# Zeros on TensorE before the first tokens, and a paced preparation, in an attention and mixture kernel

## The chip, the cores and the metric

The kernel runs on one core of one Trainium2 chip, in one launch. The metric is device time in microseconds (us), the median of several runs.

## What is computed

Two blocks follow each other. The first is a causal attention with decay in 8 heads; it has no softmax, so it is computed with a running state per head:

```python
for b in range(nb):                       # blocks of 64 positions of q, k, v [4, 8, 768, 64]
    intra = einsum('bhic,bhjc->bhij', qb, kb) * Dmask     # powers of lam below the diagonal
    intra = einsum('bhij,bhjd->bhid', intra, vb)
    inter = einsum('bhid,bhde->bhie', qb * lam_pow, kv_state)
    out[:, :, sl] = intra + inter
    kv_state = lam_block * kv_state + einsum('bhsd,bhse->bhde', kb * rev_pow, vb)
```

Its output, laid out as x [3072, 512], goes through four experts, whose results are weighted by normalised probabilities:

```python
p = domain_probs / (domain_probs.sum(-1, keepdims=True) + 1e-09)
for e in range(4):                        # w1 [4, 512, 1024], w2 [4, 1024, 512], float32
    h = np.maximum(x @ w1[e], 0.0)
    out += p[:, e:e + 1] * (h @ w2[e])
```

## The kernel before

The tokens are cut into chunks of 128 and three groups of eight chunks (group 0, 1, 2). A unit is one group with one expert: twelve units. The products of a unit are made by Strassen's scheme, seven products M1 to M7 of half-size blocks in place of eight, and each of the seven is again split so. What enters them are the blocks A11 to A22 of a weight, B11 to B22 of the tokens, and sums of those (S1 to S4, T1 to T4). The sums of weights and tokens are made on GpSimd and VectorE ahead of time, written to DRAM (`w1_ops`, `x_ops`, `w2_sums`, `w2_ops`) and fetched when their product comes.

The program writes out every engine's order itself. It starts with the loads, all issued by SyncE (SP) in this order:

```python
for n, names in ((0, "qk"), (1, "qk"), (0, "v"), (2, "qk"), (1, "v")):
    load(n, names)
raw_w1(0, "A11")
load(3, "qk")
load(2, "v")
raw_w1(0, "A12")
load(3, "v")
raw_w1(0, "A21")
raw_w1(0, "A22")
```

A chunk passes through three functions. `turn` transposes q and k on TensorE (`qp`, `kp`), ScalarE copies the results out, and GpSimd decays k. `scores` multiplies them (`sp`), VectorE masks. `values` makes the output (`op`) and the new state, which VectorE writes to `kv`; ScalarE copies the output to `xT`, the tokens of the group. For group 0 the chunks run through a loop, and quarters of the first two products of unit 0 (M1 and M2, from raw weights) stand between:

```python
between = {
    4: (m1[0], m1[2]), 5: (m2[0], m2[2]), 6: (m1[1],), 7: (m1[3],), 8: (m2[1],),
    9: (lambda: None, lambda: None, m2[3]),
}
for i in range(CPG + 2):                   # CPG = 8
    if i > 5:
        pump()
    more = list(between.get(i, ()))
    for f, lag in ((scores, 1), (turn, 0), (values, 2)):
        n = i - lag
        if 0 <= n < CPG:
            f(n, pairs[n % 3])
        if i == 9 and lag == 2:
            x_sums()                       # T1 to T4 of the tokens, VectorE
        if more:
            more.pop(0)()
    if i + 4 < CPG:
        load(i + 4)
```

Then come the other five products of unit 0, in quarters (`direct_product`, tile `pM`; M5 is the third). Preparation is a list of small jobs, `chores`. Each call of `pump` does one of them, and issues the stores of the one before the last:

```python
def pump():
    for f in older:
        f()
    older[:] = stores
    stores.clear()
    if chores:
        chores.pop(0)()
```

The rest is the loop over units. In each of its seven steps one product of the next unit's first layer (`a`, tile `pg`, operands `xs_in` and `ws_in`) and one of this unit's second layer (`b`, tile `q` with weights `w2t`; in the last group, nested once more, tile `pq`) are interleaved in parts. VectorE adds each part to its sum when TensorE has ended it, and so frees the PSUM bank. For unit 1 the preparation `own(m)` makes the sums of tokens on VectorE and those of weights on GpSimd just before use:

```python
for at, (g, e) in enumerate(units):
    ...
    for i in range(7):
        for _ in range(2 if at + i == 0 else 1):
            if fill2:
                feed2(*fill2.pop(0))       # loads w2t of this or the next product
        ...
        if nested:
            order = [a[0:2], b[0:2], a[2:4], b[2:4], a[4:6], b[4:6], a[6:8], b[6:8]]
        else:
            order = [a[0:2], b[0:1], a[2:4], b[1:2], a[4:6], b[2:3], a[6:8], b[3:5]]
        for x, part in enumerate(order):
            for f in part:
                f()
            ...
            if x == 0 and at * 7 + i >= 6 and fill:
                feed(*fill.pop(0))         # loads xs_in, ws_in of the next product
            if steps and (at > 0 or i > 1) and (x == 5 or (x == 2 and i in (1, 3, 5) and at > 0)):
                steps.pop(0)()             # attention of the next group
            if x % (2 if g == 0 else 3) == 0:
                pump()
```

Of the kernel before, what the change touches and what calls it, by code (L numbers as in the profile page):

```python
# [21 lines left out]
def kernel(  # L22
# [30 lines left out]
    nc = tc.nc  # L53
# [39 lines left out]
    def tt(eng, o, a, b, op):  # L93
        eng.tensor_tensor(out=o, in0=a, in1=b, op=op)  # L94

# [35 lines left out]


    chores, stores, older, made = [], [], [], set()

    def pump():
        for f in older:
            f()
        older[:] = stores
        stores.clear()
        if chores:  # L140
            chores.pop(0)()

    def nothing():
        pass

    def until(what):
        while what not in made:
            pump()

    def inner(eng, what, to, blk, ops, at):  # L150
# [6 lines left out]
        stores.append(lambda: (  # L157
# [24 lines left out]
    def weight_steps(block, total, ready):  # L182
        return [
            lambda: (block("A11", 0, 0), block("A21", 1, 0), block("A22", 1, 1)), nothing, nothing,
# [32 lines left out]
    def prepare_w2(e):  # L217
# [8 lines left out]
        def total(name, n, a, b, op):  # L226
# [3 lines left out]
            stores.append(lambda: (  # L230
# [6 lines left out]
            lambda: (block("B12", 0, 1), block("B22", 1, 1)), nothing,  # L237
# [11 lines left out]
    def inner_w2(e, m, blk):  # L249
# [6 lines left out]
        stores.append(lambda: (  # L256
# [80 lines left out]
    for n, names in ((0, "qk"), (1, "qk"), (0, "v"), (2, "qk"), (1, "v")):  # L337
        load(n, names)
    raw_w1(0, "A11")
    load(3, "qk")  # L340
# [3 lines left out]
    raw_w1(0, "A21")  # L344
    raw_w1(0, "A22")
# [61 lines left out]
    now = [0]  # L407
# [107 lines left out]
    def attention(g):  # L515
# [3 lines left out]
        for n in range(g * CPG, (g + 1) * CPG):  # L519
# [3 lines left out]
            def end(n=n):  # L523
                values(n, ("s0", "s1"))
# [161 lines left out]
    def first_product(g, e, m, blocks, tags):  # L686

        while (g, e, m) not in fed:
            pump()
# [55 lines left out]
    def second_product(g, e, m, banks):  # L745

        def part(sj, s):
# [29 lines left out]
            if e == E - 1 and m in ("M2", "M4", "M5", "M3"):  # L777
                stores.append(lambda: nc.sync.dma_start(out=out[n * P:(n + 1) * P, j * DH:(j + 1) * DH], in_=o))
# [218 lines left out]
    def keep_own(what, to, pieces):  # L997
        def store():
            for (x, y), of in pieces:
                nc.sync.dma_start(out=to[:, x:y], in_=of)  # L1000
            made.add(what)

        stores.append(store)
# [35 lines left out]
    def x_sums():  # L1039
        for name, a, b in (("T1", "B12", "B11"), ("T2", "B22", "T1"), ("T3", "B22", "B12"), ("T4", "B21", "T2")):  # L1040
            t = stream.tile([P, 7, 256], FP32, name="xt", tag="xw"[len(x_now) % 2])
            x_tile[name] = t
            x_now[name] = t[:, 0:4].rearrange("p (c a) t -> p c (a t)", c=2)
            tt(nc.vector, x_now[name], x_now[a], x_now[b], ALU.subtract)

    blocks = {}
    m1, m2 = (direct_product(0, m, blocks, ("g1", "g3")) for m in ("M1", "M2"))
    between = {
        4: (m1[0], m1[2]), 5: (m2[0], m2[2]), 6: (m1[1],), 7: (m1[3],), 8: (m2[1],), 9: (lambda: None, lambda: None, m2[3]),
# [151 lines left out]
```

## Time and profile before

| | |
|---|---|
| time, median of 3 runs | 1210.46 us (1207.51 to 1210.76) |
| span of the profiled execution | 1207.5 us |
| first work of TensorE | 4.64 us |
| attention of group 0 | to about 59 us |
| rest of unit 0 (direct products) | about 59 to 94 us |
| loop over units, two layers side by side | about 94 to 1153 us |
| last unit | about 1153 us to the end |
| data moved | 317.94 MB, 263 GB/s on average |

In the profile PE is TensorE's products and PEld its weight loads, DVE is VectorE, ACT ScalarE, POOL GpSimd, SP the engine that issues nearly all DMAs. A float32 product appears as two records, so a group of eight records is four products in the program. A line of the timeline gives start and duration in us, then engine, line of the kernel, operation, output and inputs, shapes and count; in square brackets stands how long the engine was idle before it and what ended that. Line L94 is a helper that records all sums of two tensors, so those are told apart by their tiles. The waits view sums such idle times: total, number, longest. The chain follows the work that ended last back to the start. DMA and queue lines (SPq) give the time in which SyncE issued, not the time of the transfer.

### The profile page before, as it was taken

What the parts mean: (1) busy time and instruction counts of PE and PEld (TensorE: products, weight loads), DVE (VectorE), ACT (ScalarE), POOL (GpSimd) and SP (SyncE); (2) the same over time, 40 slices, a digit from 0 to 9 for tenths busy, and PEclk for the clock granted to TensorE, in tenths of its full rate; (3) what the DMA queues carried; (4) which work ended last, traced back from release to release, by engine and by line L of the source; (5) the groups of instructions that cost most, each with busy time, mean ns of one, the idle gap of its engine ahead of it and who ended that gap; (6) DMA issues with size and microseconds to landing.
All of it is one profiled execution on the core that took longest, in us unless ns stands there. A gap on an engine that the chain in (4) does not pass through costs nothing.

```text
span 1207.5 us, 17884 instructions
## 1 busy us (share of the span) xinstructions
PE 1187.3 (98%) x6593; PEld 1028.4 (85%) x6593; DVE 792.4 (66%) x1313; ACT 262.1 (22%) x476; POOL 635.0 (53%) x600
## 2 busy tenths in 40 slices
PE   7999999999999999999999999999999999999998
PEld 6887888888888888888888888888888888888877
DVE  5597687478467746746765774764665667777774
ACT  3322122112212211311221120120143241241132
POOL 4664258376366900025534746405665764873873
PEclk9999999999999999999999999999999999999999
DMA  9668479999999976679987998988987667566542
GB/s 234 186 217 293 171 250 330 366 332 349 334 328 344 306 233 197 225 238 291 299 284 239 298 326 309 304 311 259 320 297 249 226 216 260 205 248 211 203 172 72
DMA packets 227448, 317.94 MB, mean 263 GB/s; under 512 B 91649, under 2 KB 168865, under 8 KB 227361
## 3 DMA queue, kind: packets, MB, share of 16 engines
q1 hardware_dynamic: 219920, 314.63, 77.1%
q10 hardware_dynamic: 7440, 2.17, 0.8%
q8 instruction: 52, 0.85, 0.3%
q14 instruction: 36, 0.29, 0.1%
HBM read 231.40 MB, written 85.34 MB: 262 GB/s over the span
## 4 chain that ended last, share of the span: by engine, by line
PE 92%; DVE 3%; DMA 2%; SPq 2%; issue 1%; ACT 0%; DVEq 0%
PE pg L706 38%; PE q L760 30%; PE pq L931 13%; PE pM L1021 3%; PE op L488 2%; PE sp L460 2%; DMA ws_in<-w_ops 1%; PE op L483 1%; DVE m L94 1%; SPq L115 1%; PE kp L437 1%; PE qp L437 1%; PE op L496 1%; DVE hS L94 1%; PE pM L901 1%
## 5 line engine op out<-in xcount | busy, mean ns | idle before, releaser
L706 PE MATMUL pg<-xs_in,ws_in 128*128 128x256 f32 x1960 | 473.2, 382 | 1.4 <-DMA ws_in<-w_ops 1.0
L706 PEld LDWEIGHTS pg<-xs_in,ws_in 128*128 128x128 f32 x1960 | 368.7, 190 | 57.9 <-DVE m L94 5.7
L94 DVE TENSOR_TENSOR m<-pg,m 128x512 f32<-128x512 f32 x451 | 307.7, 688 | 132.2 <-PE pg L706 124.1
L760 PE MATMUL q<-w2t,hS 128*128 128x256 f32 x1024 | 242.6, 380 | 0.0
L760 PEld LDWEIGHTS q<-w2t,hS 128*128 128x128 f32 x1024 | 194.3, 190 | 26.3
L776 DVE SCALAR_TENSOR_TENSOR acc<-q,gate,acc 128x256 f32<-128x256 f32 x192 | 92.5, 482 | 155.8 <-PE q L760 155.5
L760 PE MATMUL q<-w2t,m 128*128 128x256 f32 x768 | 181.9, 380 | 2.1 <-DMA w2t<-in_moe_w_dram 2.1
L760 PEld LDWEIGHTS q<-w2t,m 128*128 128x128 f32 x768 | 145.7, 190 | 22.1 <-ACT m L1033 2.5
L718 ACT ACTIVATE m<-m 128x512 f32<-128x512 f32 x132 | 82.9, 630 | 346.7 <-DVE m L94 308.7
L94 POOL TENSOR_TENSOR kn<-kn,s_decay 128x512 f32<-128x512 f32 x20 | 22.6, 1132 | 204.1 <-PE kp L437 161.8
L94 POOL TENSOR_TENSOR m<-m,xT 128x512 f32<-128x512 f32 x64 | 81.2, 1286 | 73.9 <-ACT m L718 60.4
L94 DVE TENSOR_TENSOR sums<-pq,sums 128x256 f32<-128x256 f32 x154 | 64.6, 422 | 46.8 <-PE pq L931 43.1
L931 PE MATMUL pq<-acc,w2t 128*128 128x256 f32 x352 | 86.7, 380 | 0.0
L714 ACT COPY m<-pg 128x512 f32<-128x512 f32 x88 | 51.2, 585 | 142.9 <-PE pg L706 142.8
L94 DVE TENSOR_TENSOR m<-m,m 128x512 f32<-128x512 f32 x96 | 79.3, 832 | 0.0
L931 PEld LDWEIGHTS pq<-acc,w2t 128*128 128x128 f32 x352 | 66.9, 190 | 9.4 <-issue 0.6
L94 POOL TENSOR_TENSOR ops<-w2b 128x256 f32<-128x256 f32 x24 | 18.3, 783 | 104.2 <-DMA w2b<-in_moe_w_dram 92.9
L653 ACT ACTIVATE m<-m 128x512 f32<-128x512 f32 x48 | 30.3, 631 | 147.0 <-DVE m L94 147.0
L94 POOL TENSOR_TENSOR acc<-hT,hT 128x512 f32<-128x512 f32 x32 | 40.2, 1269 | 30.7 <-PE pq L931 21.3
L94 DVE TENSOR_TENSOR hS<-m,m 128x512 f32<-128x512 f32 x64 | 52.5, 824 | 5.6 <-ACT m L718 5.6
L94 POOL TENSOR_TENSOR w2o<-w2b 128x512 f32<-128x512 f32 x32 | 42.2, 1341 | 13.0 <-DMA w2b<-in_moe_w_dram 11.2
L94 POOL TENSOR_TENSOR acc<-hT,acc 128x512 f32<-128x512 f32 x32 | 40.7, 1270 | 7.4 <-PE pq L931 5.4
(126 smaller groups left out, 1321.1 us busy)
## 6 DMA issues: line engine op xcount, KB each, us to landing
xs_in<-x_ops SPq DMA_DIRECT2D x70, 896.0 KB, 4.9
ws_in<-w_ops SPq DMA_DIRECT2D x70, 896.0 KB, 8.2
w2t<-w_ops SPq DMA_DIRECT2D x66, 256.0 KB, 6.6
w2t<-w_sums SPq DMA_DIRECT2D x64, 256.0 KB, 5.0
w_ops<-ops SPq DMA_DIRECT2D x28, 512.0 KB, 5.7
w2t<-in_moe_w_dram SPq DMA_DIRECT2D x48, 256.0 KB, 4.2
x_ops<-ops SPq DMA_DIRECT2D x17, 512.0 KB, 6.2
w2b<-in_moe_w_dram SPq DMA_DIRECT2D x32, 256.0 KB, 5.7
```

What stands on the lines that cost most here:

```text
L94: eng.tensor_tensor(out=o, in0=a, in1=b, op=op)
L437: nc.tensor.transpose(out=x[:, ac * C:(ac + 1) * C], in_=y[:, 2 * ac:2 * ac + 2].rearrange("p r d -> p (r d)"), identity=ident[:],)
L460: nc.tensor.matmul(out=sp[r][:, ac * C:(ac + 1) * C], lhsT=hc(kT)[half[r], ac], rhs=hc(qT)[half[r], ac], start=True, stop=True,)
L488: nc.tensor.matmul(out=op[r][half[x], a * C:(a + 1) * C], lhsT=vn[:, 4 * r + 2 * a + x], rhs=hc(st[r])[:, 2 * a + x], start=(first and a = ...
L653: nc.scalar.activation(out=o[:], in_=o[:], func=AF.Relu)
L706: nc.tensor.matmul(out=p[:, j * 256:(j + 1) * 256], lhsT=ws[i][:, j * P:(j + 1) * P], rhs=xs[i], start=(fresh and j == 0), stop=True, skip ...
L714: nc.scalar.copy(out=new[at][:], in_=p[:])
L718: nc.scalar.activation(out=new[at][:], in_=new[at][:], func=AF.Relu)
L760: nc.tensor.matmul(out=p[:, s * DH:(s + 1) * DH], lhsT=h[A_OF[m]][:, c * 256 + s * P:c * 256 + (s + 1) * P], rhs=fed2[g, e, m][uu][:, c], ...
L776: nc.vector.scalar_tensor_tensor(out=o, in0=x, scalar=w, in1=o, op0=ALU.mult, op1=ALU.add)
L931: nc.tensor.matmul(out=p[:, 0:256], lhsT=fed3[e, m, x // 2][:, x % 2, c * P:(c + 1) * P], rhs=b[B_OF[i]][:, c * 256:(c + 1) * 256], start= ...
L1021: nc.tensor.matmul(out=p[:, s * 256:(s + 1) * 256], lhsT=a[c][:, f:f + P], rhs=b[:, c, j * 256:(j + 1) * 256], start=(s == 0 and c == 0), ...
```

## The change

It has five parts. TensorE multiplies zeros from the start (a block of `xT` that is not in use yet), to be at full clock when the first tokens come. The first chunks are reordered: q and k of chunk 3 are loaded before the weights A11, the weights A21 and A22 come later, and in the first rounds a chunk is transposed before the scores of the one before. Two quarters of the product M5 are made in the last round of the attention, to fill its waits, and the sums T1 are split in halves for it. The preparation is paced: every job on GpSimd is counted with an estimate of how long GpSimd will be busy, the next one waits until then, and stores wait until their data should be there. In each step of the loop the part of the second layer now comes first, and w2t is fetched one product earlier.

```diff
     def tt(eng, o, a, b, op):
         eng.tensor_tensor(out=o, in0=a, in1=b, op=op)
+        if eng is nc.gpsimd:
+            busy[0] = max(busy[0], now[0]) + math.prod(o.shape[1:]) / 480
...
-    def pump():
-        for f in older:
-            f()
-        older[:] = stores
-        stores.clear()
-        if chores:
+    LEFT = 1
+    def store(f):
+        queue.append((busy[0] + 2, f))
+
+    def pump(pace=1.0, force=False):
+        while results:
+            results.pop(0)()
+        begins = chores and (force or free[0] <= now[0])
+        while queue and (force or queue[0][0] <= now[0] or begins and len(queue) > LEFT):
+            queue.pop(0)[1]()
+        if begins:
+            begin = free[0] = max(free[0], now[0] - 1)
+            was = max(busy[0], now[0])
             chores.pop(0)()
+            free[0] = max(free[0], begin + max(pace * (busy[0] - was), 1))
...
-    for n, names in ((0, "qk"), (1, "qk"), (0, "v"), (2, "qk"), (1, "v")):
+    for n, names in ((0, "qk"), (1, "qk"), (0, "v"), (2, "qk"), (1, "v"), (3, "qk")):
         load(n, names)
     raw_w1(0, "A11")
-    load(3, "qk")
     load(2, "v")
     raw_w1(0, "A12")
     load(3, "v")
-    raw_w1(0, "A21")
-    raw_w1(0, "A22")
+    zeros = xT[:, 3, G - P:]
+    nc.vector.memset(zeros, 0.0)
+    def warm(n):
+        p = bank("g1", "zp")
+        for _ in range(n):
+            nc.tensor.matmul(out=p[:, 0:P], lhsT=zeros, rhs=zeros, start=True, stop=True)
+    warm(10)
...
             def end(n=n):
+                if n == g * CPG:
+                    for m in MS:
+                        until(("x", g - 1, m))
                 values(n, ("s0", "s1"))
...
-        4: (m1[0], m1[2]), 5: (m2[0], m2[2]), 6: (m1[1],), 7: (m1[3],), 8: (m2[1],), 9: (lambda: None, lambda: None, m2[3]),
+        4: (m1[0], m1[2]), 5: (m2[0], m2[2]), 6: (m1[1],), 7: (m1[3],), 8: (m2[1],),
+        9: (m2[3], quarter_5(0), quarter_5(2)),
...
-        if i > 5:
-            pump()
-        for f, lag in ((scores, 1), (turn, 0), (values, 2)):
+        order = [(scores, 1), (turn, 0), (values, 2)]
+        if i < 3:
+            order[0:2] = order[1::-1]
+        for f, lag in order:
             n = i - lag
             if 0 <= n < CPG:
                 f(n, pairs[n % 3])
+            if i < 2 and lag == 0:
+                warm(3 - i)
+            if i == 8 and lag == 0:
+                x_sums(("T1", 0))
             if i == 9 and lag == 2:
-                x_sums()
+                x_sums(("T1", 1), *((x, y) for x in ("T2", "T3", "T4") for y in range(2)))
             if more:
                 more.pop(0)()
+            now[0] += 1
+            pump()
         if i + 4 < CPG:
             load(i + 4)
+        if i == 1:
+            raw_w1(0, "A21")
+            raw_w1(0, "A22")
...
     for m in SEQ0[2:]:
+        if m == SEQ0[-1]:
+            for _ in range(2):
+                feed2(*fill2.pop(0))
...                                        (jobs of own(m): four slots into each step)
-            for _ in range(2 if at + i == 0 else 1):
-                if fill2:
-                    feed2(*fill2.pop(0))
+            if fill2:
+                feed2(*fill2.pop(0))
...
-            if nested:
-                order = [a[0:2], b[0:2], a[2:4], b[2:4], a[4:6], b[4:6], a[6:8], b[6:8]]
+            if not ahead:
+                order = [[], b[0:2], [], b[2:4], [], b[4:6], [], b[6:8]]
+            elif nested:
+                order = [b[0:2], a[0:2], b[2:4], a[2:4], b[4:6], a[4:6], b[6:8], a[6:8]]
             else:
-                order = [a[0:2], b[0:1], a[2:4], b[1:2], a[4:6], b[2:3], a[6:8], b[3:5]]
+                order = [b[0:1], a[0:2], b[1:2], a[2:4], b[2:3], a[4:6], b[3:5], a[6:8]]
...
-                if x % (2 if g == 0 else 3) == 0:
-                    pump()
+                pump(PACE[g])              # 1.0, 1.4, 1.0
```

## The prediction

> **What bounds the kernel now.** I read the first section of the page and the chain, then the waits of TensorE, then the windows and the timeline where a wait stands.
>
> ```profile
> PE 1187.3 (98%) x6593; PEld 1028.4 (85%) x6593; DVE 792.4 (66%) x1313; ACT 262.1 (22%) x476; POOL 635.0 (53%) x600
> PE 92%; DVE 3%; DMA 2%; SPq 2%; issue 1%; ACT 0%; DVEq 0%
> ```
>
> TensorE is busy for 98% of the span and is 92% of the chain. To learn whether busy means full, I take the pace: groups of eight 128x256 products start every 1.73 us in the chain (59.16 to 93.93: 160 products in 34.77 us), which is 0.216 us each with no hole. Only holes can be won.
>
> ```profile
> PE qp L437 <- DMA qn<-in_q_dram: 4.9, 2, 4.6
> PE pg L706 <- DVE m L94: 2.5, 5, 1.2
> PE q L760 <- DMA w2t<-in_moe_w_dram: 2.1, 1, 2.1
> ```
>
> These waits (total, times, longest) are small, and the largest is at the very start. The busy time hides a second loss, seen in the timeline at the start (start, duration, group):
>
> ```profile
> 4.64 1.09 PE L437 MATMUL qp<-ident,qn 128*128 128x128 f32 x4 [4.64 <-DMA qn<-in_q_dram]
> 12.00 2.08 PE L460 MATMUL sp<-qT,kT 64*128 64x128 f32 x16 [0.67 <-ACT kT L443]
> 16.04 2.54 SPq L324 DMA_DIRECT2D w1b<-in_moe_w_dram  x4
> 17.18 1.16 PE L460 MATMUL sp<-qT,kT 64*128 64x128 f32 x16
> 24.69 0.63 PE L437 MATMUL qp<-ident,qn 128*128 128x128 f32 x4 [0.23 <-DMA qn<-in_q_dram]
> 25.56 0.63 PE L437 MATMUL kp<-ident,kn 128*128 128x128 f32 x4 [0.23 <-issue]
> ```
>
> The same scores group takes 2.08 us at 12.00 and 1.16 at 17.18: until about 15 us TensorE runs at half pace. Then the chain passes to the queue: chunk 4's q is issued at 18.62 to 19.10, behind the four weight loads of 16.04, and lands at 24.56. The other holes:
>
> ```profile
> 54.64 0.67 PE L483 MATMUL op<-qs,kv 64*64 64x128 f32 x16 [0.95 <-DVE kv L508]
> 59.16 20.96 PE L1021 MATMUL pM<-xt,w1o 128*128 128x256 f32 x96 [0.44 <-DVE xt L94]
> 95.92 1.10 PE L706 MATMUL pg<-ops 128*128 128x256 f32 x4 [0.64 <-DVE m L94]
> 99.11 1.10 PE L760 MATMUL q<-w2t,m 128*128 128x256 f32 x4 [2.09 <-DMA w2t<-in_moe_w_dram]
> 174.97 1.13 PE L706 MATMUL pg<-ops 128*128 128x256 f32 x4 [1.24 <-DVE m L94]
> ```
>
> And a small one that repeats in every step from 900 to 1145 us:
>
> ```profile
> 930.46 1.03 PE L931 MATMUL pq<-hT,w2t 128*128 128x256 f32 x4
> 930.66 0.69 DVE L94 TENSOR_TENSOR m<-pg,m 128x512 f32<-128x512 f32 x1 [0.44 <-PE pg L706]
> 931.40 2.00 PE L706 MATMUL pg<-xs_in,ws_in 128*128 128x256 f32 x8
> ```
>
> The four products at 930.46 end their slot at 931.32; the next eight reuse the bank that VectorE is still emptying (930.66 + 0.69 = 931.35), so they start at 931.40 and their first weight load is not hidden. Steps are 943.68 - 931.40 = 12.28 us apart for 56 products of 0.216 = 12.09: 0.19 us lost in each.
>
> **What the Trainium skill says.** "TensorE: Matmul & The Clock Gate", section "What's actually happening": the array idles at half clock, and a busy window of about 3.4 us releases it. The durations above agree in the factor, but here 10 us of broken activity, not 3.4, came before the change of pace (first work 4.64, fast near 15), and the granted clock of the page says 1.00 all along, so it doesn't show this. "SBUF — State Buffer", section "Who interferes with whom": a VectorE instruction with two inputs in SBUF contends with GpSimd's reads. The trace agrees: two sums hS<-m,m take 2.35 us at 65.90 beside GpSimd, and 0.68 each at 96.90 with GpSimd idle. "Perfetto Trace Analysis", section "Identifying the Most-Contended Engine": matmul busy share is a poor measure and the weight loads' share is better; that is 85% here, and the pace of 0.216 us shows the rest is not free time.
>
> **The change, part by part.**
>
> *Zeros and chunk order.* Ten zero products before the tokens, and three and two more after the transposes of chunks 0 and 1, fill time in which TensorE waits; they cost nothing on the path if they end before 4.64. The transposes of chunk n+1 now stand before the scores of chunk n, which covers the two waits of 0.67 for ScalarE. Warm costs from later rows: transposes of a chunk 0.88 (32.85 to 33.73), scores 1.09, values 2.09 (19.29 to 21.38; the first of a sequence 1.5), four products of the weights 1.73. Chunk 2's k (issued at 7.34 to 7.93, about 3.4 us to land, an estimate from the first loads) comes near 11.3. After it stand half a transposition 0.44, scores 1.09, values 1.5, scores 1.09, transposition 0.88, values 2.1, scores 1.09, products 1.73 = 9.9, so TensorE asks for chunk 4 at about 21.2. The weights A21 and A22 (four loads, 1.05 MB) now come after chunk 5: at the 313 GB/s of the window 17.2 to 22.5 that is 3.3 us, so q of chunk 4 lands near 24.56 - 3.3 = 21.2 and its k about 0.9 later. Chunk 4's second half then starts near 22.1 instead of 25.56: 3.4 us, of which I count **3.0**, as the array may warm late.
>
> *M5 in the attention.* At the end of attention TensorE works through values 6 and 7 and one quarter of M2: 52.13 to 59.16 is 7.03 us for 0.93 + 0.57 + 2.09 + 1.73 = 5.3. Now the quarter of M2 and a quarter of M5 (3.45 us) stand between values 6 and 7, and another behind them, more than the waits of 0.95 and 0.44. The moved quarters are no new work. Gain **1.7**.
>
> *Weights fetched before the loop.* 86.86 + 32 x 0.216 = 93.8 is where TensorE would be free; at 99.11 it has done eight products (1.73) since: 3.6 us lost. In the new order of the queue the first two pairs of w2t stand far ahead of the stores that wait for VectorE (they were issued at 94.63 behind them), so the 2.09 goes. VectorE's own preparation of M1 (88.27 to 91.8, 3.5 us in four sums) now follows the last evacuations instead of standing in front of them, so those are punctual; but the second group of the loop needs its first sum. Evacuation 0.2 + 0.69, two sums of 0.68 and that one put it at about 2.9 us after TensorE's end against 2.6 us of other work. I leave 1.1 of loss: gain **2.5**.
>
> *Paced preparation.* Followed through the program, the pacing meets its deadlines with two exceptions: at the end of chunk 8 all of chunk group 0's preparation is forced, so the sums for M3 and M4 come in one burst of eight on VectorE (5 to 6 us); and M5 of group 1 is stored just before it is fetched. Now four waits lie there: 1.24 at 174.97, in the windows 0.95 us idle at 220 to 260 and 0.2 at 400 to 410, with their unhidden weight loads about 3.0. I expect the burst to cost about as much as the one at 174.97, and the late fetches (ws_in after stores) to go: gain **1.4**, the least certain term.
>
> *b before a in each step.* In the last third two groups (1.73 us) instead of one (0.86) now separate the last product into a bank from the next first one, and the evacuation needs 0.9: 20 steps x 0.19 = 3.7, of which **3.0**. In the other steps one part of 0.86 remains between, so nothing there. At the last unit the final ReLU loses its cover (0.96 waited at 1153.47 already): **-0.3**.
>
> Sum: 3.0 + 1.7 + 2.5 + 1.4 + 3.0 - 0.3 = 11.3; 1210.5 - 11.3 = 1199.2.
>
> **The rivals.** (1) *Data, not clock, sets the start.* Queue and DMA are full in the first 45 us (DMA share 0.93 to 1.06 in the windows), for the same bytes. Then the zeros bring nothing, and only the chunk order counts: 1 to 2 us at the start, about 1201. For it: the chain runs through the queue. Against: chunks 6 and 7 are used at 40.56 and 46.53, after the DMA's fall to 3 GB/s at 45 to 50, so they have slack. (2) *VectorE becomes the bound* around 60 to 110 and at the burst: it is busy 19.2 of 20 us at 60 to 80. Then the waits for m and ops grow by 2 to 5 us: about 1203. Against: the sums come earlier and spread. (3) *The queue blocks.* Forced stores wait for GpSimd in order, and loads of w2t and ws_in stand behind; a step is 13 us and a load 5 to 8, so one blockage costs up to 5 us: 1204 to 1208. (4) *All holes close*: about 16 us, 1194.
>
> **Range and chances.** 1199, from 1194.5 (rival 4) to 1205.5 (rivals 2 and 3 in part). Faster by over 2% would need 24 us; the holes named here, with the first 4.64 that no zeros shorten, don't hold that. Slower by over 2% would need a blockage in many steps: 0.02. Within 2%: 0.97.
>
> **What would show it.** Scores of chunk 1 at 1.16 instead of 2.08; the transposes of chunk 4 near 22; no wait of 0.95 for kv; no wait for w2t near 95; steps of 12.09 us from 900 on; a wait for VectorE's m or ops four steps into the loop. I am wrong if the early scores stay at 2.08, if TensorE waits for ws_in or w2t past 100 us by more than 3 us in total, or if the last third still has steps of 12.28.

## The result and the profile after

The changed kernel takes **1205.3 us** (median of 6 runs, 1203.03 to 1206.49) against 1210.0 us in the same runs: ratio 0.9961, 95% interval 0.9946 to 0.9976. It is faster by 4.7 us, where the prediction had 11.3. The page's first section and the shares of the chain, as they stand after:

```profile
PE 1188.0 (99%) x6623; PEld 1031.2 (86%) x6623; DVE 793.2 (66%) x1318; ACT 261.9 (22%) x476; POOL 635.3 (53%) x600
PE 90%; DVE 3%; SPq 3%; DMA 2%; POOL 1%; issue 1%; ACT 0%; DVEq 0%; POOLq 0%
```

TensorE's share rose to 99%, though part of it is zeros: the 30 records more are the 15 zero products. The shares say nothing of the gain. The waits of TensorE do (total, times, longest):

```profile
PE pg L733 <- DVE ops L95: 2.9, 1, 2.9
PE pq L958 <- POOL acc L95: 1.9, 1, 1.9
...
PE pq L958 <- DVE sums L95: 1.1, 1, 1.1
...
PE kp L461 <- DMA kn<-in_k_dram: 0.5, 1, 0.5
```

The wait of 2.1 us for w2t is gone, and of the 2.5 us for VectorE's m 0.5 are left. In their place is one of 2.87 us for `ops`, the sums that VectorE makes for the first product M1 of unit 1. The timeline at the start (start, duration, group):

```profile
1.05 4.64 PE L368 MATMUL zp<-xT 128*128 128x128 f32 x20 [1.05 <-DVE xT L363]
5.48 1.06 PE L461 MATMUL qp<-ident,qn 128*128 128x128 f32 x4
9.13 1.16 PE L484 MATMUL sp<-qT,kT 64*128 64x128 f32 x16
15.18 2.91 SPq L122 DMA_DIRECT2D qn<-in_q_dram  x2
22.64 0.63 PE L461 MATMUL kp<-ident,kn 128*128 128x128 f32 x4 [0.48 <-DMA kn<-in_k_dram]
```

The first scores take 1.16 us at 9.13, so the array is at full pace there. The q of chunk 4 is issued at 15.18 instead of 18.62, and the chunk's second transposes start at 22.64 instead of 25.56. The zeros end only at 5.48, later than the 4.64 at which the kernel before had its first tokens.

Now the place where the gain was lost, TensorE first and VectorE below it:

```profile
94.98 1.40 PE L733 MATMUL pg<-ops 128*128 128x256 f32 x4 [2.87 <-DVE ops L95]
96.17 3.32 PE L787 MATMUL q<-w2t,m 128*128 128x256 f32 x8
99.33 1.03 PE L733 MATMUL pg<-ops 128*128 128x256 f32 x4
```

```profile
91.07 0.68 DVE L95 TENSOR_TENSOR m<-pM,m 128x512 f32<-128x512 f32 x1
91.67 1.15 DVE L95 TENSOR_TENSOR hS<-m,m 128x512 f32<-128x512 f32 x1
92.86 1.63 DVE L95 TENSOR_TENSOR hS<-hS,m 128x512 f32<-128x512 f32 x1
94.42 0.75 DVE L95 TENSOR_TENSOR ops<-xT 128x256 f32<-128x256 f32 x2
```

TensorE ended the direct products at 89.36. VectorE emptied the last of them only at 91.07, then made two sums `hS` for a later product, and only at 94.42 the sum that TensorE was waiting for. After the wait a group of eight records (what the prediction counts as eight products) takes 3.32 us instead of 1.89: the array has fallen to half pace. From 94.98 to 99.33 it makes 12 such records, 2.59 us at 0.216 each, in 4.35; so 1.76 us more are lost, 4.63 in all.

By the time at which equally many products have been started in the two profiled executions (zeros not counted), the changed kernel is ahead by:

| up to | ahead | in this stage | predicted |
|---|---|---|---|
| chunk 4 (pM at 26.02 before, 23.11 after) | 2.9 us | +2.9 | +3.0 |
| end of the direct products (about 93.77 before, 89.36 after) | 4.4 | +1.5 | +1.7 |
| first steps of the loop | 3.3 | -1.1 | +2.5 |
| 410 us | 5.7 | +2.4 | +1.4 |
| 880 us | 5.2 | -0.5 | 0 |
| end of the last full unit | 6.6 | +1.4 | +3.0 |
| end | 5.1 | -1.5 | -0.3 |

### The profile page after: what moved, and what is told of

Same layout as the page of the kernel before. It is cut to its first block, busy times and chain, and to the rows that moved or that the text cites. A ratio compares the mean times of both kernels' runs of the same rounds, so it can differ in the third digit from the quotient of the medians.

```text
span 1202.6 us, 17908 instructions
## 1 busy us (share of the span) xinstructions
PE 1188.0 (99%) x6623; PEld 1031.2 (86%) x6623; DVE 793.2 (66%) x1318; ACT 261.9 (22%) x476; POOL 635.3 (53%) x600
## 4 chain that ended last, share of the span: by engine, by line
PE 90%; DVE 3%; SPq 3%; DMA 2%; POOL 1%; issue 1%; ACT 0%; DVEq 0%; POOLq 0%
PE pg L733 38%; PE q L787 33%; PE pq L958 12%; DVE m L95 2%; SPq L122 2%; PE sp L484 1%; PE op L512 1%; POOL w2o L95 1%; PE op L507 1%; PE qp L461 1%; PE kp L461 1%; PE pM L928 1%; DMA probs<-in_moe_domain_probs_dram 1%; DMA w1b<-in_moe_w_dram 1%; PE op L520 1%
## 5 line engine op out<-in xcount | busy, mean ns | idle before, releaser
L958 PEld LDWEIGHTS pq<-acc,w2t 128*128 128x128 f32 x352 | 66.8, 190 | 11.3 <-issue 2.2
```

The costliest lines, as they stand in the source:

```text
L958: nc.tensor.matmul(out=p[:, 0:256], lhsT=fed3[e, m, x // 2][:, x % 2, c * P:(c + 1) * P], rhs=b[B_OF[i]][:, c * 256:(c + 1) * 256], start= ...
```

## The experiments

Single runs of one kernel differ by some microseconds, and a profile is one of those runs; so a median and a profile are read together. All times are medians, each ratio is to the kernel before in runs on the same chip, with its 95% interval.

| kernel | us | ratio to before | interval |
|---|---|---|---|
| after + products into the wait | 1203.79 | 0.9946 | 0.9931 to 0.9961 |
| own sums of M1 ahead | 1207.82 | 0.9986 | 0.9977 to 0.9994 |
| own sums of M1 earlier still | 1209.09 | 0.9990 | 0.9982 to 0.9999 |
| bank pairs alternate | 1205.28 | 0.9960 | 0.9946 to 0.9974 |
| own sums ahead, later jobs held ("held") | 1200.19 | 0.9921 | 0.9905 to 0.9937 |
| no zeros | 1203.03 | 0.9939 | 0.9923 to 0.9956 |
| five zeros | 1203.98 | 0.9953 | 0.9942 to 0.9964 |
| a first | 1212.31 | 1.0007 | 0.9994 to 1.0021 |
| held, no zeros | 1200.72 | 0.9907 | 0.9880 to 0.9934 |
| old chunk order | 1203.42 | 0.9929 | 0.9901 to 0.9956 |
| old chunk order, no zeros | 1206.20 | 0.9957 | 0.9941 to 0.9972 |
| M5 behind the attention | 1200.92 | 0.9912 | 0.9882 to 0.9941 |
| after, once more | 1204.62 | 0.9944 | 0.9927 to 0.9961 |
| held, pacing undone (jobs late) | 1216.86 | 1.0050 | 1.0035 to 1.0066 |
| held, M5 behind the attention | 1199.71 | 0.9908 | 0.9893 to 0.9924 |
| combined | 1198.86 | 0.9899 | 0.9884 to 0.9915 |
| held, pacing undone | 1207.33 | 0.9968 | 0.9956 to 0.9981 |
| held, M5 and M2's quarter behind | 1201.09 | 0.9917 | 0.9902 to 0.9932 |

### The wait at the loop's start

**Products into the wait.** My theory was that the wait itself throws the array to half pace. Ten products that count for nothing were put into it, into a bank that is free there:

```diff
+                    if at == 0 and i == 0 and x == 1 and y == 0:
+                        p = bank("s1", "zp")
+                        for _ in range(10):
+                            nc.tensor.matmul(out=p[:, 0:P], lhsT=ident[:], rhs=ident[:], start=True, stop=True)
```

> The changed kernel, with ten products of the identity with itself between the first and the second group of the loop's first step, where TensorE waits 2.87 us for VectorE's sums for M1. They write a bank nobody reads. Theory (the wait itself costs 2.87 us and, after it, the array runs at half pace, 3.32 us for a group of eight instead of 1.89): the group after the wait starts where it did, near 95, but the following groups run at 1.89, and the loop is 1.5 to 2 us ahead of the changed kernel from 100 us on. Rival (the slow groups after the wait are slow for another reason, such as VectorE or the loads): the groups stay at 3.3 us and the kernel is 0 to 2 us slower.

The timeline of this kernel at the same place:

```profile
91.42 2.40 PE L1220 MATMUL zp<-ident 128*128 128x128 f32 x20
94.05 1.10 PE L733 MATMUL pg<-ops 128*128 128x256 f32 x4 [0.23 <-DVE ops L95]
94.99 1.89 PE L787 MATMUL q<-w2t,m 128*128 128x256 f32 x8
```

The eight records after the wait take 1.89 us again. Behind the loop's start the trace is 2.6 us ahead of the changed kernel's and stays so, of which 0.5 was there before the loop. The mechanism is shown, and all four runs had a mean clock of 1.000; the median fell by 1.5 us only.

**The sums earlier.** Next I took away what is waited for: the own sums of M1 are recorded right behind the last evacuation, ahead of the two `hS`, and in a second kernel three quarters of a product earlier.

```diff
+            for f in raws:                 # weights of unit 1, loaded earlier for it
+                if f in chores:
+                    chores.remove(f)
+                    f()
...
+            if m == SEQ0[-1] and x == 3:   # second kernel: x == 0
+                chores.remove(mine["M1"])
+                mine["M1"]()
```

> The changed kernel with the preparation of M1 for unit 1 recorded right behind the last evacuation of unit 0, ahead of the last two background sums of VectorE (and the raw weights of unit 1 loaded one product earlier). Theory (the place in VectorE's queue makes the wait): the first sum comes about 2.4 us earlier, the wait of 2.87 falls below 1 us, the array stays at full pace, and the kernel is 3 to 4 us faster than the changed one (about 1201.5). Rival (VectorE is simply full from 57 to 95 us, whatever the order): the wait moves to the next sums or evacuations, and less than 1 us is won.

> The same, with the preparation of M1 recorded behind the first quarter of M4, as in the kernel before. Theory (the place in the queue): no wait for the sums; but the evacuations of M4 behind them are 2 to 3 us late, as before, and TensorE waits about 1 us for a bank at the start of the loop: 2 to 3.5 us faster than the changed kernel. Rival (VectorE is full): no gain, the wait only changes its name.

Both missed. The wait at 95 us was gone (the trace was 3.3 us ahead of the changed kernel at 130 us), but new ones came. VectorE's line and the wait that follows it, from the first of the two:

```profile
98.59 3.56 DVE L95 TENSOR_TENSOR xt<-xt 128x256 f32<-128x256 f32 x4
102.90 1.10 PE L733 MATMUL pg<-xT,ops 128*128 128x256 f32 x4 [1.89 <-DVE m L95]
```

Four sums stand ahead of an evacuation. In the kernel before such four took 1.80 us at 100.14, with GpSimd idle; here they take 3.56 beside it. The Trainium skill, page "SBUF — State Buffer", section "Who interferes with whom", gives a reason: a VectorE instruction with two inputs in SBUF contends with a GpSimd instruction that reads SBUF. The trace agrees that the sums slow down while GpSimd's run (from 98.55 to 101.87 here). A second wait of 2.61 us at 149.35 was followed by half pace. Both kernels end behind the changed one. But the jobs behind M1 had also moved forward, by three to five steps: the pacing starts each when the one before is done.

**The sums earlier, the rest where it was.** So one line was added that holds the next job back to the step at which the changed kernel has it:

```diff
     start, w1_steps = now[0], prepare_w1(2)
+    free[0] = max(free[0], start + 6)
```

> As in the run with the own sums of M1 ahead of the last two hS sums, but the seven later jobs are held at the places they have in the changed kernel (one added line sets the earliest place of the next job 6 steps after the loop's start). Theory: the wait of 2.87 us at the loop's start and its half pace stay away, because VectorE has the M1 sums done earlier, and the new waits near 101, 146 and 225 us came only from the later jobs having moved forward by 3 to 5 places, so they go: the kernel is 3.0 to 3.8 us faster than the changed kernel from 130 us to the end, about 1201.5 us. Rival: VectorE is simply full beside GpSimd between 57 and 150 us, so that any work taken out of one place waits in another: at least one wait of over 1.5 us for VectorE stays between 97 and 150 us, and the time stays at 1204 to 1208 us.

The windows view gives the pace that was granted from 95 to 99 us (columns: stretch, length, busy time and count of PE, PEld, DVE, ACT and POOL, granted clock, DMA share, GB/s), first for the changed kernel, then for this one:

```profile
95.00:99.00 4.00, 4.00 (x11) 3.22 (x12) 2.61 (x6) 0.58 (x1) 0.00 (x0) 0.58 0.52 206
```

```profile
95.00:99.00 4.00, 4.00 (x21) 3.51 (x20) 3.96 (x9) 1.17 (x2) 0.00 (x0) 1.00 0.82 325
```

Both show PE busy for all 4 us, but with 11 records against 21, at a clock of 0.58 against 1.00. A wait of 1.03 us is left, and no new one of over 0.5 us comes between 97 and 300 us. At 1200.19 us it is 5 us faster than the changed kernel, and the intervals of the two ratios don't meet. Its profile, the slowest of its four runs, gains 3.5 us at the loop's start, from 0.8 behind the changed kernel's at chunk 4 to 2.7 ahead at 100 us, and ends 2.2 ahead; the rest of the 5 us no trace shows. Over its whole span the granted clock was 1.000 in all four runs; of the changed kernel's eleven runs eight had 0.998, two 0.999 and one 1.000. A fall of 3.41 us to 0.50, as the trace has it, brings the mean to 0.9986, so a mean of 1.000 leaves no room for one. The kernel before has such falls too: there is none in its profile, but 41 of its 105 runs beside these experiments had 0.998 or less. This settles the failed step: the sums of M1 came too late on VectorE, and VectorE can make them earlier if nothing else moves.

### The start

```diff
-    warm(10)                               # no zeros: these two; five zeros: warm(5)
-                warm(3 - i)
```

> The changed kernel without any of its products of zeros (ten ahead, and three and two between the first chunks); the order of the chunks' steps and of the loads stays as changed. Theory: the clock sets the start, so the first scores take about 2.1 us again instead of 1.16, the transposes of chunk 4 come 1.5 to 3 us later than the changed kernel's 22.64 us, and the kernel loses 1.5 to 3 us: 1206.5 to 1208.5 us. Rival: the waits for the tokens by DMA at chunk 4 (0.22 and 0.48 us are left in the changed kernel) set the start whatever the clock, so that the slower array only uses up those waits: transposes of chunk 4 within 0.5 us of 22.64 us and the time at 1205 to 1206 us.

> The changed kernel with five products of zeros ahead instead of ten. The ten end at 5.48 us, 0.84 us after the first tokens landed at 4.64 us. Theory: five end at about 3.2 us at the cold pace, the first chunk begins at 4.64 us, the array is warm a little later or by the same 7 us, and what is gained is taken back by the wait for the tokens of chunk 4 (0.22 and 0.48 us now), so within 0.5 us of the changed kernel at chunk 4 and at the end (1204.5 to 1206 us). Rival 1: ten are too many, and the 0.84 us is gained in full: 1204.3 us. Rival 2: five are too few to warm the array, the scores of chunk 0 or 1 take 2.1 us, and 1 to 2 us are lost.

The timeline without zeros:

```profile
4.53 1.08 PE L460 MATMUL qp<-ident,qn 128*128 128x128 f32 x4 [4.53 <-DMA qn<-in_q_dram]
8.82 1.44 PE L483 MATMUL sp<-qT,kT 64*128 64x128 f32 x16
22.59 0.63 PE L460 MATMUL kp<-ident,kn 128*128 128x128 f32 x4 [0.42 <-DMA kn<-in_k_dram]
93.86 1.10 PE L732 MATMUL pg<-ops 128*128 128x256 f32 x4 [1.80 <-DVE ops L95]
94.80 1.89 PE L786 MATMUL q<-w2t,m 128*128 128x256 f32 x8
```

The rival holds. The first products do run at half pace (1.08), the array changes pace during the scores at 8.82, and chunk 4 starts at 22.59 as with zeros, because its tokens come then. What was gained came at the loop's start (1.80 us of wait and no half pace after it): the trace is 0.1 us ahead of the changed kernel's at 80 us and 2.8 at 100, the median 2.3. Why the wait is shorter here is not shown; the changed kernel itself had 2.87 us in one profile and 2.41 in another. To learn whether the zeros do harm in themselves, they were taken out of the kernel with the held jobs:

> The kernel with the own sums of M1 ahead and the later jobs held, without any product of zeros. Theory: the zeros are worth nothing in either direction (without them chunk 4 was transposed at 22.59 us instead of 22.64), and the 2.3 us that the changed kernel gained without its zeros came at the loop's start alone, where its wait was 1.80 us instead of 2.87 and no half pace followed; here that wait is gone already, so the time stays within 0.6 us of the 1200.2 us with zeros. Rival: the zeros cost some 2 us in themselves, by a way the trace does not show, and the kernel falls to 1197.5 to 1198.5 us.

1200.72 against 1200.19 us: nothing. With five zeros the last ended at 3.55, a microsecond before the tokens came at 4.51; the first scores took 1.27 us at 10.83, chunk 4's second transposes came at 23.20, and in that execution the wait at the loop was 3.41 us. Its 20 runs span 1201.0 to 1209.3, so the 1.3 us in the median against the changed kernel says little.

Then the order of the chunks, undone alone and together with the zeros, so that in the second kernel only the new order of the loads is left:

```diff
-        if i < 3:
-            order[0:2] = order[1::-1]
```

> The changed kernel with the order of the first three chunks' steps undone alone (scores of the chunk before ahead of the transposes of the next); zeros and the order of the loads stay. Theory: the transposes of the next chunk fill the time in which the scores wait for the copies of the transposed tokens, so without them holes come back among the first three chunks: the second transposes of chunk 4 (22.64 us in the changed kernel) come 1 to 2 us later, and the time is 1206 to 1207.5 us. Rival: with the zeros the array is warm either way and the tokens' transfers set chunk 4, so it stays within 0.5 us of 22.64 us and the time at 1204.5 to 1206 us.

> The changed kernel with both the zeros and the order of the first chunks undone; of the change to the start only the new order of the loads is left. Theory: either of the two is enough to have the array at full pace by 9 or 10 us, and without both it is at half pace until 13 to 15 us as in the kernel before: the second transposes of chunk 4 at 24.5 to 25.6 us instead of 22.64, 2 to 3 us lost, 1207 to 1208.5 us. Rival: the start was won by the loads alone (tokens of chunk 3 and 4 ahead of weights): chunk 4 by 23.2 us and the time at 1203 to 1206 us.

The first kernel starts the second transposes of chunk 4 at 22.78: with zeros the order is worth nothing that shows. The second, with neither:

```profile
7.32 2.08 PE L483 MATMUL sp<-qT,kT 64*128 64x128 f32 x16 [0.68 <-ACT kT L466]
11.97 1.16 PE L483 MATMUL sp<-qT,kT 64*128 64x128 f32 x16 [0.68 <-ACT kT L466]
23.13 0.60 PE L460 MATMUL kp<-ident,kn 128*128 128x128 f32 x4
```

The holes and the half pace are back, and still chunk 4 comes at 23.13. So of the 2.92 us (25.56 to 22.64) the loads alone bring 2.43 in this execution; my theory for this run, 24.5 to 25.6, was wrong. Whether zeros and order bring the last 0.5 can't be told: in the thirteen profiles of kernels that share the changed kernel's start, the same transposes come anywhere from 21.97 to 23.96. And one thing stays open. Here the pace changed just before 12 us, in the kernel before only at about 15.4, with the same two holes. Had it come as late here, 1.8 us more would be lost (an estimate, half of the 3.6 us) and chunk 4 would come near 24.9, so that the loads alone would bring some 0.6 us. No run shows that case.

### The end of the attention

```diff
-        9: (m2[3], quarter_5(0), quarter_5(2)),
+        9: (m2[3],),                               # M5 wholly behind the attention
...
+        9: (lambda: None, lambda: None, m2[3]),    # a further kernel: M2's quarter back too
```

> The changed kernel with the two quarters of M5 taken out of the attention's end and back behind it, nothing else. Theory: the array then waits again at the attention's end for the last chunk's evacuations, as in the kernel before: 1.2 to 1.8 us lost by the last direct product, but the later array leaves VectorE as much more time, so that the wait for the own sums of M1 at the loop's start (2.87 us) and its half pace shrink by about as much: 0 to 1 us lost in all, 1205 to 1206.3 us. Rival: VectorE's work is delayed by the same amount as the array, the wait at the loop's start stays 2.5 us or more, and the whole 1.3 to 1.8 us shows in the time: 1206.5 to 1207.2 us.

> Own sums of M1 ahead and later jobs held, and M5 back behind the attention. Theory: M5's two quarters in the attention gain nothing (without them the direct products ended at the same time to 0.01 us, since moving M2's last quarter and the first sum of T1 forward had already closed the attention's end), and what the changed kernel without them gained, some 4 us in the median, is a shorter wait at the loop's start; with that wait gone anyway the time is the same as with M5 inside, 1199.7 to 1201 us. Rival: M5 inside costs VectorE something lasting (its sums of m meet GpSimd's), and 1198 to 1199.2 us is reached.

> As the kernel with own sums of M1 ahead, later jobs held and M5 behind the attention (1199.7 us), with M2's last quarter put back behind the last chunk's values, where it stood before the change. Theory: it is M2's quarter ahead of the last chunk's values, and not M5, that closed the attention's end: the wait for kv (0.95 us in the kernel before) comes back near 52 us, the direct products end 0.9 to 1.4 us later, and the time is 1200.6 to 1201.2 us. Rival: the earlier first sum of T1 and VectorE's earlier freedom closed it: no wait of over 0.4 us there, and 1199.3 to 1200.1 us.

Without M5 in it the attention ends as early: the direct products end at 89.35 instead of 89.36. Neither theory had that. With M2's last quarter put back behind the last chunk's values, the kernel before's wait returns:

```profile
53.05 0.67 PE L507 MATMUL op<-qs,kv 64*64 64x128 f32 x16 [0.95 <-DVE kv L532]
```

From chunk 4's second transposes to the end of the direct products it takes 67.54 us, where the changed kernel and both kernels with only M5 behind take 66.7 and the kernel before 68.2. The median rises by 1.4 us against the held kernel with M5 behind (1199.71 to 1201.09, on two chips), but the intervals overlap. So M2's quarter, moved forward, closed the wait for kv and is worth 0.8 us; the other 0.7 stays when it is put back, and goes with the sums T1 in halves, whose wait (0.44 for `xt`) doesn't return, though that was not undone by itself. M5 adds nothing: inside or behind, the held kernel takes 1200.2 and 1199.7 us. That the changed kernel without M5 fell to 1200.92 us must then come from the loop's start. But in its one profile the wait there is 2.46 us with half pace after it, and that was the slowest of its four runs (1203.75; the others 1199.9 to 1201.2). Two of the others had a mean clock of 1.000, so they had no fall to half pace; that their wait was shorter is inferred from this, not seen.

### Order within a step, banks, and pacing

```diff
-                order = [b[0:2], a[0:2], b[2:4], a[2:4], b[4:6], a[4:6], b[6:8], a[6:8]]
+                order = [a[0:2], b[0:2], a[2:4], b[2:4], a[4:6], b[4:6], a[6:8], b[6:8]]
...                                                  (and likewise in the loop)
```

> The changed kernel with the order of its two interleaved products undone alone (first product of the next unit ahead of the quarter of the second product, as before the change), in the loop and in the nested part. Theory: the nested steps take 12.28 us again instead of 12.09 (20 steps, 3.7 us lost), the three waits of the nested part under b-first (0.51 us at 975, 0.44 at 1044 and at 1129) go (1.2 us given back), and the wait at the last unit shrinks from 1.85 to 0.9 us: about 1.5 to 2.5 us slower than the changed kernel, 1206.8 to 1207.8 us. Rival: the 0.19 us per step was made by something else (the evacuation behind, on ScalarE or GpSimd), and the steps stay at 12.1: then the time falls by 1 to 2 us, to 1203.5 to 1204.5 us.

It lost 7 us instead of 2. In the nested part the theory held. In the changed kernel the steps there are about 12.09 us apart:

```profile
927.67 1.89 PE L733 MATMUL pg<-xs_in,ws_in 128*128 128x256 f32 x8
939.75 1.89 PE L733 MATMUL pg<-xs_in,ws_in 128*128 128x256 f32 x8
```

With a first they are 12.16 to 12.28 us again, some up to 12.42. From its first step there to the last, the execution takes 245.1 us against 243.9, so b first is worth 1.2 us. At the last unit it gives that back: with a first TensorE waits 0.96 and 0.47 us there, with b first 1.85 and 1.07. The rest of the loss lies where I expected nothing. In this kernel's timeline, of the slowest of its twelve runs:

```profile
97.36 2.05 PE L733 MATMUL pg<-ops 128*128 128x256 f32 x4 [5.03 <-DVE ops L95]
410.41 3.43 PE L733 MATMUL pg<-xs_in,ws_in 128*128 128x256 f32 x8 [2.70 <-DMA ws_in<-w_ops]
```

At the loop's start b first puts a quarter of 1.73 us ahead of the product that waits for VectorE; without it the wait is 5.03. At 410 us a fetch of weights comes late, again with half pace behind it.

For the wait of 0.51 us at 974 us, where the last product of a unit and the first of the next share a pair of banks:

```diff
-                b = nested_product(..., (...)[i % (2 if ahead else 3)])
+                b = nested_product(..., (...)[(at + i + 1) % 2 if ahead else i % 3])
```

> The changed kernel with the two pairs of banks of the last group's second layer alternating across units too (in the changed kernel the last product of a unit and the first of the next use the same pair). Theory (the second layer first puts only one group between the two users of that bank at a change of unit): the wait of 0.51 us for ScalarE's sums near 974 us goes, and that of 1.85 near 1149 shrinks by up to 0.5: 0.5 to 1.2 us faster than the changed kernel. Rival (those waits are for late operands from GpSimd): they stay, within 0.3 us of the changed kernel.

The wait is gone, and the trace gains 0.65 us there; but at the last unit the array then waited 2.12 us instead of 1.85, and the median did not move.

The pacing, undone in the loop of the held kernel:

```diff
-                pump(PACE[g])
+                if x % (2 if g == 0 else 3) == 0:
+                    pump()                 # one job, stores two places later
```

> The kernel with the own sums of M1 ahead of the last background sums, with the pacing of the loop undone alone: one job at every second or third step whether GpSimd is behind or not, one pause for two places, stores two places later, the jobs of units 3 and 0 given out where they were before the change. Theory: the pacing took away the four waits of the kernel before between 100 and 410 us (2.9 us in all, of which 0.6 us are left elsewhere), so without it 2 to 3 us are lost against the 1200.2 us of the paced one with the same loop start: 1202 to 1203.5 us. Rival: those waits were made by the order of a and b, or by where the kernel before stood, and not by the pacing: within 0.8 us of 1200.2 us.

> The run with the pacing undone lost 13.5 us near 178 to 212 us because it was no true undoing: three pauses too many put the sums of unit 2's weights some ten steps late. Here every job of the loop stands at the step at which the kernel before has it; own sums of M1 ahead of the last background sums as in the paced kernel of 1200.2 us. Theory: the four waits of the kernel before between 100 and 410 us were made by its pace and come back, 2 to 3 us lost: 1202 to 1203.5 us. Rival: they were made by the order of a and b or by where the kernel before stood: within 0.8 us of 1200.2 us.

The first of these says nothing of the pacing: with three pauses too many, the stores of unit 2's weights came late, and TensorE waited 8.31 us for them at 205.66. It only shows that a job of the loop has little slack. In the second every job stands where the kernel before has it. VectorE, then TensorE:

```profile
164.64 3.54 DVE L95 TENSOR_TENSOR xt<-xt 128x256 f32<-128x256 f32 x4
```

```profile
168.93 1.57 PE L745 MATMUL pg<-ops 128*128 128x256 f32 x4 [2.61 <-DVE m L95]
170.29 1.91 PE L745 MATMUL pg<-ops,w1o 128*128 128x256 f32 x4
```

Four sums beside a busy GpSimd, an evacuation behind them, a wait of 2.61 us and half pace after it; and later one of 1.02 for `ws_in`. The trace falls back by 6.3 us between 146 and 440 us, the median by 7.1 (ratio 0.9968 against 0.9921). So the pacing is worth more than the 1.4 us predicted and the 2.4 read from before and after: at the place where the kernel before waited 1.24 us, the same four sums (2.74 us there, 3.54 here) with an earlier array now cost a wait that is long enough for half pace.

### Once more, and combined

> The changed kernel itself once more, beside the others of this group, so that they are compared on the same chip. Theory: the wait at the loop's start with its half pace is in nearly every run of it (mean granted clock under 1.000), 1204 to 1206 us. Rival: it was the luck of one chip, half of the runs have a clock of 1.000, and the median is 1201 to 1203 us.

> Put together: own sums of M1 ahead and later jobs held; no zeros; M5 behind the attention; pairs of banks that alternate across the units of the nested part; and a ahead of b in the last two steps of the nested part's last full unit. Theory: 1200.2 us, less 0.65 us for the banks (the wait of 0.51 us at 974 us), less 0.6 to 0.9 us at the last unit, whose first third product then has its operands earlier; zeros and M5 count nothing: 1198.5 to 1199.2 us. Rival: what the last unit waits for is GpSimd's own pace and not its operands, the wait of 1.85 us stays as it did with the other banks, and the time is 1199.5 to 1200.5 us.

The changed kernel again had the wait and half pace (2.41 us in its profile; four of five runs with a clock under 1.000) and took 1204.62 us. The combined kernel takes **1198.86 us** beside it: held jobs, no zeros, M5 behind the attention, alternating banks, and a ahead of b in the last two steps before the last unit. The intervals, 0.9884 to 0.9915 and 0.9927 to 0.9961, don't meet: it beats both kernels. Its wait at the last unit is 1.11 us instead of 1.85, and the next one 0.47 instead of 1.07; a new one of 0.78 us for m stands at 1117.60. Against the held kernel with M5 behind (1199.71) the intervals overlap.

## Why the prediction was wrong

The direction was right and the time lies just inside the range, at its upper end. By the steps:

- **Start (3.0; found 2.9).** The size was right, the cause mostly not. The zeros did what they were for (full pace from about 7 us instead of 15), but without them chunk 4 came no later in three profiles: rival 1, data and not clock, fits best. Its figure of 1 to 2 us was too low for the one profile with the loads alone, 2.4. That the loads would do if the pace changed as late as in the kernel before is not shown. The estimate of when chunk 4's q lands (21.2) was good: its transposes started at 21.54.
- **M5 in the attention (1.7; found 1.5).** The size nearly right, the cause not: M2's quarter filled the hole of 0.95, and M5 nothing. I had counted the two as one move, and had not asked whether the first was enough.
- **Loop start (2.5; found -1.1): the step that failed**, by 3.6 us. The w2t wait did go. I had put the first own sum at "about 2.9 us after TensorE's end": 0.2 + 0.69 for the evacuation, two sums of 0.68, and its own 0.68. It came at 5.6 (89.36 to 94.98). The evacuation started 1.7 us after the end and not 0.2, as VectorE was behind: the array had become 4.4 us earlier, VectorE's work had not (its sums `xt`, all but the first half of T1, start at 57.30, before at 57.59). That was the change's own doing: the quarters of M2 and M5 stand ahead of the last chunk's values, for whose output these sums wait, so the values began at 54.36, before at 54.64; with M5 behind them `xt` starts at 55.57. The two sums `hS` took 2.75 us beside GpSimd, not 1.36. In the second profile of the changed kernel the last evacuation started only 0.7 us late, but the two `hS` took 2.3 and the sum itself 1.6, and it came 5.2 us after the end: the slow sums beside GpSimd are in both profiles, VectorE's backlog in one. And a consequence that stood in no step, half pace after the wait, added 1.76. Together 4.63 us of loss where I had left 1.1: 3.5 of the 3.6. The held kernel, with the sums of M1 ahead of the two `hS`, has no fall and wins 3.5 us there.
- **Paced preparation (1.4; found 2.4, and about 6 when undone alone).** Right sign, too small. The burst that I feared cost no wait of over 0.2 us.
- **b before a (3.0; found 1.4).** Steps of 12.09 did come, where 20 of them would give 241.8 us, but the execution needs 243.9: 2.1 us went at three places, the shared bank pair at 974 (0.51 us waited) and VectorE's m beside GpSimd near 1044 and 1129 (0.28 and 0.27, each with weight loads that are then not hidden). "In the other steps nothing" was wrong at the loop's first step, where the wait is 2 us shorter with b first.
- **Last unit (-0.3; found -1.5).** Mis-sized: the wait is not for one ReLU but for GpSimd's `acc`, 1.85 us, and then for VectorE's `sums`, 1.07. With a first both are back at 0.96 and 0.47, so it is the order b before a that costs this, as predicted, but five times as much.

Rival 2, VectorE as the bound, is what happened between 60 and 97 us; its 1203 us was nearer than the sum.

## What to carry to other kernels

When the array is made earlier, ask for each engine that serves it whether its work becomes earlier too; if not, write out its whole queue, at the durations it has beside its neighbour, up to the first result that is waited for. A wait after which the array falls to half pace costs 1.6 to 1.8 times itself here (2.87 became 4.63, and 2.13 became 3.9), so two short waits should be better than one long one, though no run tested that. Filling a hole of one engine can make another engine's work later, as M5 did to VectorE's sums. Filling an idle stretch with products is worth nothing where the work behind it is waiting for data anyway, as at the start. Moving one job in a paced list moves all that follow: hold the rest in place, or the experiment measures something else.

## What the runs showed of the hardware

- After a wait TensorE falls to half pace for some time if the wait was long enough. Behind the attention no wait of up to 2.12 us was followed by half pace (the longest: 1.80, 1.85, 1.89, 1.90, 2.09, 2.12), and every longer one was (2.13, 2.41, 2.46, 2.48, 2.55, 2.61, 2.70, 2.87, 3.15, 3.41, 5.03, 8.31).
- The granted clock shows this fall: it stands at 0.50 from 95.65 to 99.06 us in the changed kernel, which makes 0.58 from 95 to 99. Each fall before the kernel's end lasts 3.41 us, or 6.83 (after 3.41, 5.03 and 8.31 us of wait), and the stretches at 1.00 between the clock's changes are whole multiples of 3.41 too (in the changed kernel 88.75 us before the fall is 26 of them, 1102.5 behind it 323). So the clock seems to be set anew every 3.41 us. Counted in these stretches, all 14 falls follow one with 2.10 us or more of waiting in it, and no stretch with up to 1.85 was followed by a fall; the waits of 2.09 and 2.12 us lay across two (1.80 and 1.34 us in the fuller one). Whether a wait of about 2 us brings a fall is then a matter of where it lies. The Trainium skill, page "TensorE: Matmul & The Clock Gate", section "What's actually happening", gives an idle window of about 3.4 us for this. The length agrees; but 2.10 us of waiting in it was enough, and the measurement decides.
- The slow start does not show in the views, which print 1.00 there, because the traces have no record of the clock before its first change: this is at 15.39 us in the kernel before, 6.90 in the changed one, 9.44 without zeros, where the durations change too.
- Half-pace work warms the array by itself. With nearly continuous work from about 4.5 us the clock changed at 8.44, 9.44 and 9.66 in the three kernels without zeros; with two holes of 0.68 us at 11.77, and in the kernel before, with two of 0.67, at 15.39. So the holes alone don't set the time.
- Four VectorE sums of two tensors from SBUF (128x256 each) took 1.80 us with GpSimd idle, and 2.74, 3.12, 3.54 and 3.56 beside it, in different kernels: up to 1.8 us more in front of an evacuation that TensorE waits for.
